# The normalisation's reciprocal root: from twelve VectorE instructions to a logarithm and an exponential on ScalarE and a Newton step on GpSimd

## The chip, the cores and the metric

The kernel runs on one core of a Trainium2 chip. The metric is the device time of one execution in microseconds (us); the time before is the median of three runs. The engines' names in the profile: PE is the tensor engine's matmuls and PEld its weight loads, DVE is VectorE, ACT is ScalarE, POOL is GpSimd, SP is SyncE, which issues most transfers. Each engine works through its own instructions in the order in which they were issued, and waits where an operand or a buffer isn't ready.

## What is computed

An attention over 8 batches of 12 heads, with 448 tokens and 64 columns a head, feeds a mixture of 8 experts. Queries and keys are normalised by their root mean square first:

```python
def rmsnorm(x, g):
    rms = np.sqrt(np.mean(x * x, axis=-1, keepdims=True) + 1e-06)
    return x / rms * g
q_n, k_n = (rmsnorm(q, g_q), rmsnorm(k, g_k))
scores = scale * np.matmul(q_n, k_n.transpose(0, 1, 3, 2))
scores = scores - np.max(scores, axis=-1, keepdims=True)
attn = np.exp(scores)
attn = attn / (np.sum(attn, axis=-1, keepdims=True) + 1e-09)
attn @ v
```

Then each of the 3584 tokens is given to the expert with the largest gate logit, and goes through that expert's two matrices with a relu between them. All is in float32, and the matmuls that need it split their operands in two parts.

## The kernel before

**Units and slots.** The attention works in 48 units of two heads (u = 0 to 47), and each unit in 7 slots, one for each chunk of 128 of the two heads' tokens. A slot issues the transposed scores of a chunk (`st`, L849), their exponential on ACT, and, for a unit two ahead, the plain scores of a chunk (`sa`, L821 and L816), of which DVE takes the row maxima (TENSOR_REDUCE at_hlw<-sa). Attention times values (`av`, L888), sums, gates and the transposes of finished rows lie between them. The PSUM pools of `st` and `sa` have two buffers each, so PE can be two chunks ahead of ACT's exponentials and of DVE's maxima.

**The normalisation.** For a unit to come, queries and keys are loaded (tile r), squared on ACT (`sumsq`, xrw<-r) and summed over 64 columns on DVE (TENSOR_REDUCE at_hlw<-xrw). The sums of three units make one group of 2 x 24 columns on 112 partitions. `rstd` computes 1/sqrt(sum/64 + 1e-6) of a group: on DVE, one instruction for the mean, two on integers for a first guess, and three Newton steps of three instructions each, so twelve. Eighteen such calls are made: five at the start on parts of groups (8, 16 or 24 columns for queries and as many for keys), thirteen later on whole groups of 48 columns. The result y is multiplied onto queries and keys by POOL (`norm`, xrw<-r,at_hlw), PE transposes what comes out (`tr`, L750), and ACT and DVE evacuate it into the matmul operands w1w, w2ha and xw, which SP's transfers complete (L763).

The sums, y and the scratch a and z of `rstd` are all views of one tile, at_hlw in the profile; the scratch has one buffer.

**The order of the work.** It is written by hand. A table (PLAN) sets the slot of each step: the squares of a unit 50 and 49 slots before its own start, `rstd` of a group 48 slots before its last unit, the norms 26 slots before a unit. A call that is "deferred" doesn't go out at once: its engine calls become items in a queue, and `pump` takes some 1 to 2 items per slot from it, from L52; other calls of these engines go out from L51. `rstd` goes into the queue `fast`. The routing of finished batches (one-hot of the largest logit, positions, slot tables: some 25 small DVE instructions a batch, also from L52) goes into the queue `slow`, which moves only while `fast` is empty. From unit 36 on three items go out per slot.

**After the attention** come the slots of the experts (ph at L480, py at L510), which PE fills without a break for most of the time, and an end of small slots that wait for indirect transfers.

**Other work of the engines in the attention.** ACT also squares, copies the transposes and evacuates av; POOL also adds up the exponentials (`csum`, r2w and others, 112 to 128 partitions by 448) and issues the indirect transfers of the routing.

Of the kernel before, what the change touches and what calls it, by code (L numbers as in the profile page):

```python
# [8 lines left out]
F32 = mybir.dt.float32  # L9
F32R = mybir.dt.float32r  # L10
I32 = mybir.dt.int32
AF = mybir.ActivationFunctionType
# [25 lines left out]
class Deferred:  # L38
    """Engine calls go out at once, or into the open queue."""
# [17 lines left out]
def deferred(fn):  # L57
    """What fn issues, as queue items."""
    Deferred.queue = items = []
    fn()  # L60
    Deferred.queue = None
    return items
# [3 lines left out]
def kernel(  # L66
# [16 lines left out]
    PE, SY = nc.tensor, nc.sync  # L83

# [8 lines left out]
    # ---------------------------------------------------------------- constants  # L93
# [22 lines left out]
    V.memset(half[64:128, 1:2], 1.0)  # L116
    V.memset(wg, 0.0)
# [61 lines left out]
    # ---------------------------------------------------------------- slot tables  # L179
# [20 lines left out]
    def tables(nm, ns, cnt, nb, taken, e_prev, half_blocks=None):  # L200
# [7 lines left out]
        if taken is not None:  # L208
            # blocks of at most half the size go last: columns of their own
            br = slice(NE, nv)  # L210
            nb_e = nb
            nb, cnt_e, cnt = tl("nb", [128, nv]), cnt, tl("cnt", [128, nv])
            V.scalar_tensor_tensor(out=nb[:, br], in0=nb_e, scalar=2.0, in1=half_blocks, op0=ALU.mult,
                                   op1=ALU.subtract)
            V.tensor_tensor(out=nb[:, ar], in0=nb_e, in1=nb[:, br], op=ALU.subtract)
            V.tensor_tensor(out=nb[:, ar], in0=nb[:, ar], in1=taken, op=ALU.subtract)
            for c in (ar, br):
                V.tensor_copy(out=cnt[:, c], in_=cnt_e)
# [44 lines left out]
        if taken is not None:  # L263
            # tokens of the slot
# [26 lines left out]
    def lists(nm, s0, ns, tb, two):  # L291
# [16 lines left out]
        def fin(a, n):  # L308
# [8 lines left out]
            if two:  # L317
                # the halves of a row
# [6 lines left out]
    # ---------------------------------------------------------------- storage  # L325
    # The same tiles serve the attention and then the experts.
# [13 lines left out]
    # These hold float32 first and then split operands.  # L340
# [21 lines left out]
    # 64 columns of zeros lie between the heads  # L362
# [13 lines left out]
    # one chunk of queries: 64 of each head, a block of rows and columns each  # L376
# [39 lines left out]
    # ---------------------------------------------------------------- experts  # L416
# [126 lines left out]
    def half_slot(s):  # L543
        """A slot of at most 128 tokens: these stay in the array, and the weights move."""
# [27 lines left out]
    def small_slot(s, xr):  # L572
        """A slot of at most 32 tokens, in a quarter of the array's columns: four column blocks at once."""
# [16 lines left out]
        # gate and row of a token, for each of its four pieces  # L590
# [49 lines left out]
    # ---------------------------------------------------------------- attention  # L640
    if True:
# [12 lines left out]
        def load_v(hb):  # L654
# [3 lines left out]
            # a partition's tokens lie next to each other, but for the middle chunk  # L658
# [48 lines left out]
        def rstd(hb, j0, j1):  # L707
            t = HB[hb]
            if "y" not in t:
# [5 lines left out]
            V.tensor_scalar(out=a, in0=t["ss"][:, :, sl], scalar1=1.0 / D, scalar2=1e-6,  # L715
                            op0=ALU.mult, op1=ALU.add)
            V.tensor_scalar(out=z.bitcast(I32), in0=a.bitcast(I32), scalar1=1,
                            scalar2=None, op0=ALU.arith_shift_right)
            V.tensor_scalar(out=y.bitcast(I32), in0=z.bitcast(I32), scalar1=-1,
                            scalar2=0x5F3759DF, op0=ALU.mult, op1=ALU.add)  # L720
            for _ in range(3):
                V.tensor_tensor(out=z, in0=y, in1=y, op=ALU.mult)
                V.scalar_tensor_tensor(out=z, in0=z, scalar=-0.5, in1=a,
                                       op0=ALU.mult, op1=ALU.mult)
                V.scalar_tensor_tensor(out=y, in0=z, scalar=1.5, in1=y,
                                       op0=ALU.add, op1=ALU.mult)
# [15 lines left out]
        def tr(u, g):  # L742
# [3 lines left out]
            # keys in their own order, queries by chunk of the load  # L746
# [55 lines left out]
        # Both heads' tokens on one axis, cut in chunks of 128: the middle one has an end of each.  # L802
        def columns(t, j):
            """Head and columns of the chunk's tokens."""
# [52 lines left out]
        def csum(u, h):  # L857
# [5 lines left out]
            # the middle chunk's rows of this head, and the first of its chunks  # L863
# [32 lines left out]
        # Four units at a time, each in its 32 columns of the array: the gate's products of both  # L896
        # heads in rows 0 to 15, the sums of the exponentials in rows 16 and 17.
# [153 lines left out]
        # slots between what gives the operands and the call  # L1051
# [39 lines left out]
        wps = ps_o.tile([128, 512], F32, tag="o", name="warm")  # L1091
        load(0)
# [5 lines left out]
        # engine calls of the slots to come, before and after the slot's exponential  # L1098
# [20 lines left out]
        # what each slot does; the first units follow each other more closely  # L1119
# [148 lines left out]
        # the last units' ends, among the first slot's products  # L1268
        after = []

        def go(*fs):
            """Issue the calls; what a call returns (evacuations) goes out after the next one."""
# [46 lines left out]
        # the slots: the next one's operands are made among the products of this one  # L1319
# [6 lines left out]
        for s in range(NSTAT):  # L1326
            # calls after the products of a beat
# [114 lines left out]
```

## Time and profile before

| | |
|---|---|
| median of 3 runs | 1171.19 us (1169.7 to 1174.05) |
| span of the profiled execution, first to last instruction | 1169.2 us |
| what lies between the median and this span | 2.0 us |
| mean granted clock of the tensor engine | 0.969 |
| start, until the first st | 38.1 us |
| attention, 48 units | 38.1 to 622 us |
| experts and end | 622 to 1169 us |

The page gives the busy time of each engine and its share of the span; a row of a group of instructions reads line, engine, operation, output<-inputs, shapes, count, busy us, mean ns of one, and the idle time of the engine ahead of them with what ended it. The profiled execution's own time isn't among the figures, only its span; the table sets the span against the median of the runs.

### The profile page before, as it was taken

To read this page: it belongs to the slowest core of one execution; us is meant where nothing else is said; L and a number is where in the kernel's file an instruction comes from. 1 tells how busy PE (TensorE), PEld (TensorE's weight loads), DVE (VectorE), ACT (ScalarE), POOL (GpSimd) and SP (SyncE) were. 2 spreads that over 40 slices of the span, in tenths; PEclk is the share of its full clock that TensorE was granted. 3 is DMA by queue.
4 is the path that set the end of the run, shared out by engine and by line. 5 is a ranking of instruction groups with operands and counts; after the bars stand their busy time and mean duration, and the time that the engine had idled before them with its cause. 6 is when DMAs were issued, how large, how long until landed. Compare 5 with 4: busy or idle time off the path is not lost.

```text
span 1169.2 us, 19997 instructions
## 1 busy us (share of the span) xinstructions
PE 1105.2 (95%) x6678; PEld 865.2 (74%) x6678; DVE 954.4 (82%) x1812; ACT 815.7 (70%) x1569; POOL 635.6 (54%) x575
## 2 busy tenths in 40 slices
PE   8899999999989999898899999999999999999993
PEld 6555665655556555455457898999999999999991
DVE  6987889999999999899978996778677777767770
ACT  6677878777767777575566764787666877667770
POOL 3467666777567775566665456533344324454340
PEclk8899999999999999898899999999999999999997
DMA  7655557666566665454354121111153111111260
GB/s 186 148 134 144 146 152 180 166 161 153 139 141 166 164 156 142 121 138 105 102 176 157 63 42 55 52 32 54 29 217 108 42 55 42 28 55 55 69 217 17
DMA packets 101345, 131.78 MB, mean 113 GB/s; under 512 B 29979, under 2 KB 95983, under 8 KB 99696
## 3 DMA queue, kind: packets, MB, share of 16 engines
q1 hardware_dynamic: 83588, 88.57, 30.2%
q0 software_dynamic: 17616, 41.80, 11.2%
q8 instruction: 57, 0.93, 0.4%
q14 instruction: 56, 0.46, 0.2%
q10 hardware_dynamic: 28, 0.01, 0.0%
HBM read 148.74 MB, written 22.38 MB: 146 GB/s over the span
## 4 chain that ended last, share of the span: by engine, by line
PE 65%; DVE 19%; DMA 6%; ACT 4%; issue 2%; POOL 1%; SPq 1%; ACTq 0%; DVEq 0%
PE ph L480 17%; PE py L510 16%; PE st L849 10%; PE av L888 9%; DVE at_hlw L51 4%; PE sa L821 4%; DMA lt<-l_d,tb_li 3%; DVE at_hlw L52 3%; DVE w1w L51 3%; DVE xw L51 2%; PE tr L750 2%; PE px L463 2%; PE xt L945 2%; DMA w1w<-xw 1%; PE sm L903 1%
## 5 line engine op out<-in xcount | busy, mean ns | idle before, releaser
L480 PE MATMUL ph<-xw,w1w 128*128 128x256 f32 x2016 | 247.5, 284 | 3.0 <-DVE hlw L51 2.3
L480 PEld LDWEIGHTS ph<-xw,w1w 128*128 128x128 f32 x2016 | 245.3, 193 | 5.1 <-DVE hlw L51 2.5
L51 DVE TENSOR_TENSOR w1w<-r,w1w 128x256 fp32r<-128x256 f32 x360 | 220.8, 671 | 14.1 <-ACT w1w L51 14.0
L51 ACT CAST w1w<-r 128x256 fp32r<-128x256 f32 x360 | 224.9, 726 | 0.0
L51 DVE TENSOR_REDUCE at_hlw<-sa 128x1 f32<-128x448 f32 x336 | 205.3, 615 | 17.0 <-PE sa L821 11.7
L849 PE MATMUL st<-w1w 128*128 128x448 f32 (+1 forms) x480 | 193.9, 453 | 1.9 <-ACT r2w L51 1.4
L849 PEld LDWEIGHTS st<-w1w 128*128 128x128 f32 (+1 forms) x480 | 108.2, 241 | 45.9 <-ACT r2w L51 19.3
L821 PE MATMUL sa<-w1w 128*128 128x448 f32 (+1 forms) x288 | 114.9, 400 | 22.6 <-DVE at_hlw L51 22.3
L51 POOL TENSOR_TENSOR r2w<-r2w 128x448 f32<-128x448 f32 (+1 forms) x72 | 82.6, 1148 | 81.1 <-DVE r2w L51 33.6
L51 ACT ACTIVATE hhw<-ph 128x512 fp32r<-128x512 f32 x56 | 33.5, 598 | 124.5 <-PE ph L480 124.5
L51 POOL TENSOR_TENSOR xrw<-r,at_hlw 112x512 f32<-112x512 f32 x95 | 97.6, 1048 | 36.9 <-PE tr L750 11.2
L510 PE MATMUL py<-w2lw,hhw 128*128 128x384 f32 x448 | 113.8, 334 | 0.0
L51 ACT ACTIVATE r2w<-st 128x448 f32<-128x448 f32 x168 | 89.3, 541 | 33.3 <-PE st L849 30.4
L849 PE MATMUL st<-w1w,w2ha 65*128 65x448 f32 x288 | 102.4, 376 | 0.0
L51 ACT ACTIVATE at_w2lw<-st 128x448 f32<-128x448 f32 x168 | 87.9, 540 | 12.1 <-PE st L849 10.3
L51 ACT CAST w1w<-tr 64x448 fp32r<-64x448 f32 x96 | 50.5, 526 | 65.3 <-DVE xw L51 64.7
L51 POOL DMA_INDIRECT out_dram<-yw,lb_oi x22 | 26.7, 1214 | 122.2 <-ACT yw L51 112.3
L51 POOL TENSOR_TENSOR r2w<-r2w,at_w2lw 64x448 f32<-64x448 f32 (+1 forms) x48 | 54.8, 1142 | 66.7 <-DVE r2w L51 38.9
L821 PEld LDWEIGHTS sa<-w1w 128*128 128x128 f32 (+1 forms) x288 | 56.9, 198 | 35.2 <-DVE at_hlw L51 32.4
L51 DVE SCALAR_TENSOR_TENSOR hlw<-ph,hhw 128x512 fp32r<-128x512 f32 x56 | 38.7, 691 | 53.2 <-ACT hhw L51 53.2
L510 PEld LDWEIGHTS py<-w2lw,hhw 128*128 128x128 f32 x448 | 80.9, 188 | 0.0
L51 ACT ACTIVATE w1w<-tr,gs 64x448 fp32r<-64x448 f32 x96 | 60.3, 628 | 29.1 <-DVE xw L51 28.4
(296 smaller groups left out, 2414.2 us busy)
## 6 DMA issues: line engine op xcount, KB each, us to landing
w1w<-xw SPq DMA_DIRECT2D x312, 112.0 KB
r<-in_q_dram SPq DMA_DIRECT2D x48, 224.0 KB
r<-in_k_dram SPq DMA_DIRECT2D x48, 224.0 KB
w2ha<-xw SPq DMA_DIRECT2D x72, 112.0 KB
x_d<-at_w2hb SPq DMA_DIRECT2D x8, 672.0 KB
x_d<-yw SPq DMA_DIRECT2D x8, 672.0 KB
r2w<-in_v_dram SPq DMA_DIRECT2D x16, 288.0 KB
at_w2lw<-in_v_dram SPq DMA_DIRECT2D x16, 288.0 KB
```

Of the source, the lines that this page charges most:

```text
L51: return fn(*a, **kw)
L52: Deferred.queue.append((self.kind, lambda: fn(*a, **kw)))
L463: PE.transpose(ps[:, i, 128 * t : 128 * t + 128], xr[t][:, 2 * g + i], idn)
L480: PE.matmul(ps[:, i], lhsT=lt_, rhs=rt_[:, c], start=n == 0, stop=n == 17)
L510: PE.matmul(ps[n][:, :384], lhsT=lt_[:, j, 128 * t : 128 * t + 128], rhs=rt_[:, 384 * n : 384 * n + 384], start=j == 0 and m == 0, stop=j ...
L750: PE.transpose(sp[:, c], src[:, c], idn[:CP, :CP])
L821: PE.matmul(ps[:, :S], lhsT=t["qq"][r, h, a : a + 128], rhs=t["kk"][h][r], start=True, stop=True)
L849: PE.matmul(ps[:, :S], lhsT=l, rhs=t["qq"][:, h] if first else t["ql"][:, h], start=first and (j != 3 or h == 0), stop=not first and (j != ...
L888: PE.matmul(t["av"][64 * h : 64 * h + 64, :S], lhsT=vv[r, u % 3, j], rhs=t["p"][r, j], start=c == 0, stop=c == 3)
L903: PE.matmul(R[g][32 * i : 32 * i + 32, :S], lhsT=sel[:, m], rhs=T[u + i // 2]["cs"][:, i % 2], start=m == 0, stop=False, tile_position=(0, ...
L945: PE.transpose(ps[:CP, 128 * c : 128 * c + 128], T[u]["xt"][:, c * CP : (c + 1) * CP], idn)
```

## The change

`rstd` keeps its inputs, its output and its place in the plan. The twelve DVE calls become two on ACT and five on POOL. The logarithm is taken of sum/64 times 2^-44 plus 1e-6 times 2^-44, the exponential of -1/2 times that, less 22 ln 2, which takes the factor back out. One Newton step on POOL follows: a = sum/64 + 1e-6, z = y*y, z = z*a, z = 1.5 - z/2, y = y*z. Two constants for the activations' bias (tile lnb) are set at the start on DVE. POOL's calls go through a new Deferred object (GP), so that they are queue items as well. A call names the table set "natural_log_exp_and_others" for ACT ahead of the first load.

```diff
+    GP = Deferred(nc.gpsimd, "op")
...
+    lnb = cp.tile([128, 2], F32, name="lnb")
+    V.memset(lnb[:, 0:1], 1e-6 * 2.0**-44)
+    V.memset(lnb[:, 1:2], -22.0 * math.log(2.0))
...
             y = t["y"][:, :, sl]
-            V.tensor_scalar(out=a, in0=t["ss"][:, :, sl], scalar1=1.0 / D, scalar2=1e-6,
-                            op0=ALU.mult, op1=ALU.add)
-            V.tensor_scalar(out=z.bitcast(I32), in0=a.bitcast(I32), scalar1=1,
-                            scalar2=None, op0=ALU.arith_shift_right)
-            V.tensor_scalar(out=y.bitcast(I32), in0=z.bitcast(I32), scalar1=-1,
-                            scalar2=0x5F3759DF, op0=ALU.mult, op1=ALU.add)
-            for _ in range(3):
-                V.tensor_tensor(out=z, in0=y, in1=y, op=ALU.mult)
-                V.scalar_tensor_tensor(out=z, in0=z, scalar=-0.5, in1=a,
-                                       op0=ALU.mult, op1=ALU.mult)
-                V.scalar_tensor_tensor(out=y, in0=z, scalar=1.5, in1=y,
-                                       op0=ALU.add, op1=ALU.mult)
+            ss = t["ss"][:, :, sl]
+            A.activation(out=z, in_=ss, func=AF.Ln, scale=2.0**-44 / D, bias=lnb[:CP, 0:1])
+            A.activation(out=y, in_=z, func=AF.Exp, scale=-0.5, bias=lnb[:CP, 1:2])
+            GP.tensor_scalar(out=a, in0=ss, scalar1=1.0 / D, scalar2=1e-6, op0=ALU.mult, op1=ALU.add)
+            GP.tensor_tensor(out=z, in0=y, in1=y, op=ALU.mult)
+            GP.tensor_tensor(out=z, in0=z, in1=a, op=ALU.mult)
+            GP.tensor_scalar(out=z, in0=z, scalar1=-0.5, scalar2=1.5, op0=ALU.mult, op1=ALU.add)
+            GP.tensor_tensor(out=y, in0=y, in1=z, op=ALU.mult)
...
+        A.preload_act_table_set("natural_log_exp_and_others")
```

In the changed kernel the deferred calls go out from L53 and the others from L52.

The order of the instructions shows what moves. First ACT at the very start, before: two squares of each of units 0, 1 and 2, then the first evacuation of a transpose (w1w<-tr).

```order
L51 ACT_TABLE_LOAD
L51 ACTIVATE xrw_132<-r1_1_131 112x512
L51 ACTIVATE xrw_132<-r1_0_130 112x512
L51 ACTIVATE xrw_132<-r1_1_131 112x512
L51 ACTIVATE xrw_132<-r1_0_130 112x512
L51 ACTIVATE xrw_132<-r1_1_131 112x512
L51 ACTIVATE xrw_132<-r1_0_130 112x512
L51 ACTIVATE w1w_133<-tr0_1_216,gs_78 64x448 x2
```

And of the change, from the same place:

```order
L52 ACT_TABLE_LOAD
L52 ACTIVATE xrw_135<-r1_1_134 112x512
L52 ACTIVATE xrw_135<-r1_0_133 112x512
L52 ACTIVATE xrw_135<-r1_1_134 112x512
L52 ACTIVATE xrw_135<-r1_0_133 112x512
L53 ACTIVATE at_hlw_144<-at_hlw_144,lnb_89 112x16
L53 ACTIVATE at_hlw_144<-at_hlw_144,lnb_89 112x2x8
L52 ACTIVATE xrw_135<-r1_1_134 112x512
L52 ACTIVATE xrw_135<-r1_0_133 112x512
L53 ACTIVATE at_hlw_144<-at_hlw_144,lnb_89 112x32
L53 ACTIVATE at_hlw_144<-at_hlw_144,lnb_89 112x2x16
L52 ACTIVATE w1w_136<-tr0_1_215,gs_78 64x448 x2
```

The logarithm and the exponential of unit 0 stand behind the squares of unit 1, and those of units 1 and 2 ahead of the first evacuation. Each list has this one table load and no other.

Second, DVE in the steady part, while it takes the row maxima of unit 12 (at_hlw<-sa12); the rows at_hlw<-at_hlw of 48 columns are a root. Before:

```order
L51 TENSOR_REDUCE at_hlw_141<-sa12_3_1759 128x1
L52 TENSOR_SCALAR at_hlw_141<-at_hlw_141 112x48
L51 TENSOR_TENSOR xw_134<-tr13_0_1761,xw_134 128x448
L52 TENSOR_TENSOR at_hlw_141<-at_hlw_141 112x48
L51 TENSOR_REDUCE at_hlw_141<-sa12_4_1779 128x1
L52 SCALAR_TENSOR_TENSOR at_hlw_141<-at_hlw_141 112x48
L51 TENSOR_TENSOR yw_137<-xt4_1783,rs1_144 112x4x128
L52 SCALAR_TENSOR_TENSOR at_hlw_141<-at_hlw_141 112x48
L51 TENSOR_REDUCE at_hlw_141<-sa12_5_1804 128x1
L52 TENSOR_TENSOR at_hlw_141<-at_hlw_141 112x48
L51 TENSOR_REDUCE at_hlw_141<-sa12_6_1818 128x1
```

Of the change:

```order
L52 TENSOR_REDUCE at_hlw_144<-sa12_3_1728 128x1
L52 TENSOR_TENSOR xw_137<-tr13_0_1730,xw_137 128x448
L52 TENSOR_REDUCE at_hlw_144<-sa12_4_1748 128x1
L52 TENSOR_TENSOR yw_140<-xt4_1752,rs1_147 112x4x128
L52 TENSOR_REDUCE at_hlw_144<-sa12_5_1773 128x1
L52 TENSOR_REDUCE at_hlw_144<-sa12_6_1787 128x1
L53 TENSOR_REDUCE lo0_1794<-at_hlw_144 112x32
```

The root's rows are gone from between the maxima, and the first row of the routing (lo0) stands there already. Counted over the whole order, the routing's one-hot matmuls of batches 0 to 5 come one to three units earlier on PE; the routing's and tables' rows that DVE has in units 36 to 43 were 8, 0, 16, 6, 0, 16, 21 and 15, and are 3, 9, 10, 3, 9, 21, 21 and 1. SP's order is the same.

Third, POOL at a place of the same kind: norms (xrw) and adds of exponentials (r2w, at_w2lw). Before:

```order
L51 TENSOR_TENSOR xrw_132<-r1_0_130,at_hlw_141 112x2x4x64
L51 TENSOR_TENSOR xrw_132<-r1_1_131,at_hlw_141 112x2x4x64
L51 TENSOR_TENSOR r2w_135<-at_w2lw_139 128x448
L51 TENSOR_TENSOR r2w_135<-r2w_135,at_w2lw_139 64x448
L51 TENSOR_TENSOR at_hhw_140<-r2w_135,at_w2lw_139 128x448
L51 TENSOR_TENSOR r2w_135<-r2w_135,at_w2lw_139 128x448
```

Of the change:

```order
L52 TENSOR_TENSOR xrw_135<-r1_0_133,at_hlw_144 112x2x4x64
L52 TENSOR_TENSOR xrw_135<-r1_1_134,at_hlw_144 112x2x4x64
L53 TENSOR_SCALAR at_hlw_144<-at_hlw_144 112x48
L52 TENSOR_TENSOR r2w_138<-at_w2lw_142 128x448
L53 TENSOR_TENSOR at_hlw_144<-at_hlw_144 112x48 x2
L52 TENSOR_TENSOR r2w_138<-r2w_138,at_w2lw_142 64x448
L53 TENSOR_SCALAR at_hlw_144<-at_hlw_144 112x48
L52 TENSOR_TENSOR at_w2lw_142<-r2w_138,at_w2lw_142 128x448
L53 TENSOR_TENSOR at_hlw_144<-at_hlw_144 112x48
L52 TENSOR_TENSOR r2w_138<-r2w_138,at_w2lw_142 128x448
```

The five steps stand between the adds, one or two at a time; each adds to POOL's row, and the second waits for ACT's exponential.

More of the change, by code (lines that the diff above doesn't have):

```diff
@@ L1 @@
+import math
 from contextlib import ExitStack
```

## The prediction

> **What bounds the kernel now.** I read the page first: the engines' busy shares and the chain that ended last.
>
> ```profile
> span 1169.2 us, 19997 instructions
> PE 1105.2 (95%) x6678; PEld 865.2 (74%) x6678; DVE 954.4 (82%) x1812; ACT 815.7 (70%) x1569; POOL 635.6 (54%) x575
> PE 65%; DVE 19%; DMA 6%; ACT 4%; issue 2%; POOL 1%; SPq 1%; ACTq 0%; DVEq 0%
> PE ph L480 17%; PE py L510 16%; PE st L849 10%; PE av L888 9%; DVE at_hlw L51 4%; PE sa L821 4%; DMA lt<-l_d,tb_li 3%; DVE at_hlw L52 3%; DVE w1w L51 3%; DVE xw L51 2%; PE tr L750 2%; PE px L463 2%; PE xt L945 2%; DMA w1w<-xw 1%; PE sm L903 1%
> ```
>
> PE carries the chain, but 19% of it runs over DVE, and 3% (some 35 us) over "DVE at_hlw L52". L52 is the place from which queued work is issued, and at_hlw written there by DVE is this very root. To find where it binds I cut the span into the start, the attention and its end; each row of a window gives its length, then PE, PEld, DVE, ACT and POOL busy in us (and instructions), the granted clock, the share of DMA and GB/s. The second fence has the same stretches for the st matmuls alone (L849); a unit (two heads) issues 16 of them, so the counts give units.
>
> ```profile
> 0.00:38.10 38.10, 31.58 (x187) 27.46 (x188) 26.80 (x83) 25.37 (x94) 14.28 (x30) 0.87 0.72 181
> 38.10:77.80 39.70, 33.34 (x143) 20.42 (x141) 36.94 (x71) 26.73 (x63) 23.57 (x22) 0.87 0.51 126
> 87.50:233.40 145.90, 145.90 (x767) 87.27 (x765) 128.41 (x258) 116.96 (x252) 99.86 (x91) 1.00 0.62 158
> 233.40:463.40 230.00, 220.84 (x1134) 131.23 (x1132) 219.56 (x433) 169.63 (x370) 157.12 (x145) 0.99 0.62 151
> 463.40:580.80 117.40, 103.34 (x482) 59.98 (x480) 107.14 (x223) 68.33 (x150) 74.44 (x70) 0.90 0.46 114
> 580.80:622.00 41.20, 41.20 (x219) 24.74 (x217) 31.18 (x55) 30.33 (x61) 29.83 (x26) 1.00 0.56 171
> ```
>
> ```profile
> 38.10:77.80 39.70, 17.02 (x48) 10.76 (x48) 0.87 0.51 126
> 87.50:233.40 145.90, 67.83 (x208) 43.25 (x208) 1.00 0.62 158
> 233.40:463.40 230.00, 100.27 (x304) 63.72 (x304) 0.99 0.62 151
> 463.40:580.80 117.40, 44.16 (x128) 27.88 (x128) 0.90 0.46 114
> ```
>
> From 87.5 to 233.4 us PE is busy all the time, at the full granted clock, while DVE is busy 128 of 146 us. That is the floor: 208/16 = 13 units in 145.9 us, 11.22 us each, and a lighter DVE can bring nothing there. Above the floor stand three stretches. The first three units take 39.7 us, 6.0 over 3 x 11.22. The next 304/16 = 19 units take 230.0, 16.8 over 213.2; DVE is busy 95% of it. Then 128/16 = 8 units take 117.4, 27.6 over 89.8, and the clock falls to 0.90 because PE waits. In all **50.4 us** are DVE's doing. After 580.8 PE is full again and no root is left; the experts behind it stay as they are.
>
> How much of it is the root's? Single units show that. The first five rows below are the longest units that hold a root (7 of its 12 instructions or all); the next two hold no root, only routing work (L52 too); the last holds 7 of a root's as well.
>
> ```profile
> 257.80:271.70 13.90, 12.13 (x54) 7.39 (x52) 13.07 (x24) 9.71 (x22) 9.61 (x9) 0.88 0.58 113
> 330.30:345.70 15.40, 12.99 (x62) 7.43 (x60) 14.57 (x25) 10.12 (x23) 9.77 (x10) 0.89 0.58 108
> 403.90:416.40 12.50, 10.74 (x54) 6.61 (x52) 11.67 (x20) 9.60 (x23) 9.22 (x9) 1.00 0.62 121
> 480.80:496.40 15.60, 13.69 (x66) 8.01 (x65) 14.58 (x26) 9.48 (x22) 9.60 (x9) 0.89 0.39 92
> 521.00:537.60 16.60, 13.62 (x67) 7.79 (x65) 15.35 (x27) 9.46 (x21) 11.74 (x12) 0.89 0.27 63
> 463.40:480.80 17.40, 14.57 (x62) 8.24 (x60) 14.61 (x25) 9.20 (x21) 10.16 (x10) 0.80 0.66 168
> 550.50:567.30 16.80, 14.23 (x63) 7.67 (x61) 15.13 (x37) 7.69 (x17) 9.56 (x9) 0.80 0.49 130
> 294.80:306.70 11.90, 11.90 (x68) 7.04 (x64) 10.93 (x26) 8.56 (x19) 7.66 (x7) 1.00 0.49 124
> ```
>
> Over 11.2 us the five stand 2.7, 4.2, 1.3, 4.4 and 5.4 us, together 18.0; the two routing units 6.2 and 5.6. The last, at 11.9, hardly stands over it: a root alone does not stall PE, it does so where DVE is full besides (13.1 of 13.9 us busy in the first row) and where it meets a run of POOL work, as shown next.
>
> **What is removed.** The root's instructions on DVE, by the groups of instructions:
>
> ```profile
> L52 DVE TENSOR_SCALAR at_hlw<-at_hlw 112x48 int32<-112x48 int32 (+5 forms) x54 | 42.0, 777 | 0.4
> L52 DVE SCALAR_TENSOR_TENSOR at_hlw<-at_hlw 112x48 f32<-112x48 f32 (+2 forms) x108 | 37.1, 344 | 1.5
> L52 DVE TENSOR_TENSOR at_hlw<-at_hlw 112x48 f32<-112x48 f32 (+2 forms) x54 | 19.9, 368 | 0.8
> ```
>
> Eighteen roots of 12 instructions: 216, and 42.0 + 37.1 + 19.9 = 99.0 us of DVE. That is far more than 48 columns need, and the order of time shows why:
>
> ```profile
> 484.92 2.04 POOL L51 TENSOR_TENSOR xrw<-r,at_hlw 112x512 f32<-112x512 f32 x2
> 485.05 3.27 DVE L52 TENSOR_SCALAR at_hlw<-at_hlw 112x48 f32<-112x48 f32 x2
> 486.92 1.12 POOL L51 TENSOR_TENSOR r2w<-at_w2lw 128x448 f32<-128x448 f32 x1
> 488.98 0.21 DVE L52 TENSOR_TENSOR at_hlw<-at_hlw 112x48 f32<-112x48 f32 x1
> 489.22 1.89 DVE L52 SCALAR_TENSOR_TENSOR at_hlw<-at_hlw 112x48 f32<-112x48 f32 x1
> ```
>
> Two small instructions last 3.27 us and end only as a run of POOL instructions ends; the next takes 0.21 us with POOL quiet. So DVE stands still behind POOL, with the row maxima that PE's next sa needs queued behind it. These stalls go with the instructions. Late next is PE itself, at the floor, and in some units DVE's routing work, which keeps such stalls.
>
> **What is added.** ACT gets 36 small instructions, POOL 90, DVE two memsets at the start (nothing). Nearest rows:
>
> ```profile
> L52 ACT ACTIVATE lo<-lo 112x32 f32<-112x32 f32 x7 | 1.6, 231 | 0.1
> L51 ACT ACTIVATE xw<-tr,gs 128x448 fp32r<-128x448 f32 x48 | 30.2, 629 | 3.6 <-PE tr L750 3.4
> 34.57 0.20 POOL L51 TENSOR_TENSOR at_hlw<-xrw 112x8 f32<-112x8 f32 x1
> 32.10 2.39 POOL L51 TENSOR_TENSOR xrw<-xrw 112x256 f32<-112x256 f32 x5 [13.10 <-ACT xrw L51]
> ACT w1w L51 <- DVE xw L51: 93.0, 90, 5.2
> L51 ACT ACT_TABLE_LOAD x1 | 1.3, 1283 | 0.8 <-PEq L1428 0.8
> ```
>
> An activation of 48 columns lies between 0.23 (32 columns) and 0.63 us (448); it is nearest to the first, so 0.25: 36 x 0.25 = 9 us of ACT in all. ACT is idle 230.0 - 169.6 = 60 us in the 19 units, 3.2 us each; a root's 0.5 us per three units hides there. On POOL a dependent step lies between 0.20 (8 columns) and 2.39/5 = 0.48 us (mean of 256 down to 16); I take 0.3. Five make 1.5 us per root, 27 us in all (18 to 43), against 230.0 - 157.1 = 73 us idle in the 19 units, 11 per root: hidden too. Neither addition can gain by itself, since it only adds work; without its cover each would cost its own 9 or 27 us.
>
> Two waits are new. The logarithm waits in ACT's queue for DVE's sum of squares; behind it stand the exponentials of st, for which PE waits two tiles later (two buffers). In the steady part it is issued a slot after that sum, so I charge nothing; the bounds are nothing and, by the wait row above (ACT for DVE), a mean of 93.0/90 = 1.03 us, inside the 3.2. POOL's second instruction waits for ACT's exponential; behind it stand the adds for the sums and the norms, which have units of lead. SP's queue is unchanged.
>
> At the **start** ACT is not free:
>
> ```profile
> 6.38 0.59 DVE L52 TENSOR_SCALAR at_hlw<-at_hlw 112x16 f32<-112x16 f32 x3
> 8.33 1.15 ACT L51 ACTIVATE xrw<-r 112x512 f32<-112x512 f32 x2 [2.78 <-DMA r<-in_k_dram]
> 8.94 2.04 POOL L51 TENSOR_TENSOR xrw<-r,at_hlw 112x512 f32<-112x512 f32 x2 [2.83 <-DVE at_hlw L52]
> 11.84 1.25 ACT L51 ACTIVATE w1w<-tr,gs 64x448 fp32r<-64x448 f32 x2
> ```
>
> The first root ran on DVE from 6.38 and the norms from 8.94. Now the logarithm stands behind the squares of unit 1, which wait for a load until 8.33 and end at 9.48. Two activations (0.5) and four POOL steps (1.2) end at 11.2: the norms start 2.2 us late, and the second root's pair stands before the first evacuation (11.84). The root of units 3 to 5 gives part of it back. I charge 2 us, between 0 and 4.
>
> **The sum.** The five root units: 18.0, less about 2 for routing left in them, 16 (11 to 18). The other 16.8 - 8.2 = 8.6 us of the 19 units: half, 4.5, since the roots' last instructions and routing share them (2 to 8). The other 27.6 - 9.8 = 17.8 of the eight: 3 (0 to 8); here routing, which moves up into freed places, still fills two units. The first three units: 5 of 6.0 (3 to 6). Less 2 at the start: **26.5 us** saved, bounds 12 to 40. The profiled span of 1169.2 becomes 1142.7; the median 1171.2 lies 2.0 above the span, so 1144.7, say **1144.5**.
>
> **Rivals.** *Routing takes over*: with the root gone its instructions sit closer, and stall behind POOL in the same way. For it: 6.2 and 5.6 us over in units without a root. Half of the five units' 16, none of the rest but 5.5 early, less 2: about 12 saved, 1159. *All of DVE's excess goes but the two routing units and the start*: 50.4 - 11.8 - 2 = 36.6 saved, 1134.5; for it the 35 us of the root in the chain. *ACT binds instead*, no change, about 1170: against it, 74% busy where DVE is at 95%. *Slower*: the logarithm holds ACT's queue for a late DVE sum, PE starves for exponentials. Price: what exceeds 3.2 us of ACT's idle time a unit, 18 times; it decides when the mean hold passes 3.2 + 26.5/18 = 4.7 us. At the longest such wait seen, 5.2, it loses 18 x 2.0 = 36 and ends at 1180.7. *Not what it says*: if the two functions needed a table load each, 36 x 1.283 = 46 us more on ACT, 1191 with none hidden; but the changed order lists one load, as before.
>
> The Trainium skill ("ScalarE: Activation LUTs", Table sets) puts a change of set at about 2.66 us with its drain, 96 us for 36 and 1240 in all with nothing hidden, and names one set with both functions; the one row of a load here, 1.283 us, agrees with its load alone.
>
> **Chances.** Forecast (savings of 20 to 33) 0.55; routing 0.22; all of it 0.12; no change 0.06; slower 0.05 (table loads 0.01 of it). Range 1130 to 1162: it takes in the forecast, nearly all of the routing case and most of the best one. A measurement of this kernel tells about 0.5%, 6 us, from no change: faster by more 0.89, within 0.06, slower 0.05.
>
> **What would show it.** DVE's at_hlw rows of L52 gone; the stretches behind 233.4 nearer 11.2 us a unit, at a full clock; idle of PE's sa behind DVE at_hlw much smaller; the first norms near 11 us. Wrong if ACT's rows for lnb show waits of microseconds, if POOL's 48-column steps last over 1 us, or if routing rows stretch where the root stood.

## The result, and the profile after

| | before | after |
|---|---|---|
| median, us | 1172.62 (4 runs, 1169.7 to 1177.33) | 1144.11 (4 runs, 1139.65 to 1144.52) |
| span of the profiled execution, us | 1169.2 | 1137.9 |
| mean granted clock | 0.969 | 0.980 |

The ratio is 0.9748, with a 95% interval of 0.97 to 0.9796: faster by 28.5 us in the medians. The prediction said 1144.5. The profiled execution of the changed kernel took 1139.65 us and was the shortest of its four, so a sum made on the two spans, 31.3 us, is some 3 us more than the medians give.

Two lines of the page of the changed kernel, span and busy times:

```profile
span 1137.9 us, 19896 instructions
PE 1089.8 (96%) x6678; PEld 856.9 (75%) x6678; DVE 863.7 (76%) x1598; ACT 827.7 (73%) x1605; POOL 656.8 (58%) x665
```

DVE lost 954.4 - 863.7 = 90.7 us of busy time and 214 instructions (216 of the roots less two memsets); ACT got 12 and POOL 21 us. PE's busy time fell too, by 15.4 us with the same 6678 matmuls: matmuls that run at half clock count longer, and there are fewer of those.

The stretches of the prediction, cut at the first st of the same units (start; units 0 to 2; unit 3; 4 to 16; 17 to 35; 36 to 43), in the changed kernel. Columns as before: length, PE, PEld, DVE, ACT and POOL busy, granted clock, DMA share, GB/s:

```profile
0.00:37.70 37.70, 29.12 (x187) 25.96 (x188) 20.00 (x49) 25.98 (x91) 16.29 (x44) 0.91 0.73 178
37.70:77.70 40.00, 34.44 (x144) 21.28 (x142) 26.50 (x47) 28.84 (x75) 27.09 (x33) 0.83 0.50 120
87.40:233.40 146.00, 145.53 (x768) 87.03 (x766) 114.44 (x216) 119.94 (x263) 107.88 (x118) 1.00 0.64 158
233.40:454.00 220.60, 217.35 (x1134) 129.90 (x1132) 185.39 (x351) 174.14 (x382) 167.83 (x178) 0.99 0.66 157
454.00:550.30 96.30, 93.62 (x483) 54.98 (x481) 82.50 (x191) 70.23 (x153) 71.92 (x75) 0.98 0.60 140
```

Against the rows of before: the start 38.1 to 37.7; the first three units 39.7 to 40.0, no gain; units 4 to 16 145.9 to 146.0, the floor as foretold; units 17 to 35 230.0 to 220.6; units 36 to 43 117.4 to 96.3, more than two thirds of the whole gain in 8 of 48 units. In the four stretches of the attention PE's idle time (length less PE) went from 6.4 + 0 + 9.2 + 14.1 = 29.7 to 5.6 + 0.5 + 3.3 + 2.7 = 12.1 us. The clock gave back the rest: length times (1 - granted clock) is 5.2 + 0 + 2.3 + 11.7 = 19.2 before and 6.8 + 0 + 2.2 + 1.9 = 10.9 after. Together the stretches are 30.1 us shorter. These two numbers explain some 26 of that: 18 were waits, and 8 a lower granted clock.

The five units that held a root, at the new places:

```profile
257.70:267.90 10.20, 10.20 (x54) 6.50 (x52) 8.67 (x18) 9.33 (x22) 8.49 (x11) 1.00 0.57 139
327.60:338.70 11.10, 11.10 (x62) 6.64 (x61) 8.56 (x17) 9.46 (x22) 9.02 (x13) 1.00 0.59 146
398.10:408.40 10.30, 10.30 (x55) 6.54 (x53) 8.77 (x19) 9.43 (x22) 8.56 (x12) 1.00 0.58 139
465.80:477.10 11.30, 11.30 (x62) 6.74 (x61) 9.15 (x22) 9.65 (x22) 8.00 (x12) 1.00 0.68 163
500.30:512.50 12.20, 11.74 (x63) 6.74 (x62) 8.34 (x21) 8.87 (x20) 9.28 (x13) 1.00 0.49 106
```

They took 74.0 us and take 55.1: 18.9 saved. Four have PE busy from end to end at a full clock. DVE, busy 11.7 to 15.4 us in each before, is busy 8.3 to 9.2.

The groups of instructions that the change adds, and two that waited for the root (line, engine, operation, count | busy, mean ns | idle before and what ended it); the last row is the matmuls sa in the kernel before:

```profile
L53 ACT ACTIVATE at_hlw<-at_hlw,lnb 112x48 f32<-112x48 f32 (+2 forms) x36 | 11.7, 326 | 1.5 <-DVE at_hlw L52 0.9
L53 POOL TENSOR_TENSOR at_hlw<-at_hlw 112x48 f32<-112x48 f32 (+2 forms) x54 | 15.9, 294 | 11.9 <-ACT at_hlw L53 9.8
L53 POOL TENSOR_SCALAR at_hlw<-at_hlw 112x48 f32<-112x48 f32 (+2 forms) x36 | 8.1, 224 | 9.9 <-DVE at_hlw L52 5.6 <-DVE bs L53 2.4 <-DVE gs L52 0.4
L823 PE MATMUL sa<-w1w 128*128 128x448 f32 (+1 forms) x288 | 110.6, 385 | 8.9 <-DVE at_hlw L52 5.8 <-DMA w1w<-xw 2.6 <-issue 0.3
L52 POOL TENSOR_TENSOR xrw<-r,at_hlw 112x512 f32<-112x512 f32 x95 | 97.4, 1045 | 2.5 <-PE tr L752 2.2
L821 PE MATMUL sa<-w1w 128*128 128x448 f32 (+1 forms) x288 | 114.9, 400 | 22.6 <-DVE at_hlw L51 22.3 <-ACT w1w L51 0.3
```

ACT's pair costs 0.33 us an instruction where 0.25 was taken, and waits 1.5 us for all 36: the wait that the slower rival needed is not there. POOL's 90 steps come to 15.9 + 8.1 = 24.0 us, 0.27 each (taken: 0.3). PE's idle time ahead of sa is 8.9 us, 5.8 of it behind DVE; it was 22.6, 22.3 of it behind DVE.

### The profile page after: what moved, and what is told of

It reads as the page before. It is cut to its first block, busy times and chain, and to the rows that moved or that the text cites. A ratio compares the mean times of both kernels' runs of the same rounds, so it can differ in the third digit from the quotient of the medians.

```text
span 1137.9 us, 19896 instructions
## 1 busy us (share of the span) xinstructions
PE 1089.8 (96%) x6678; PEld 856.9 (75%) x6678; DVE 863.7 (76%) x1598; ACT 827.7 (73%) x1605; POOL 656.8 (58%) x665
## 3 DMA queue, kind: packets, MB, share of 16 engines
q0 software_dynamic: 17616, 41.80, 11.7%
## 5 line engine op out<-in xcount | busy, mean ns | idle before, releaser
L52 DVE TENSOR_REDUCE at_hlw<-sa 128x1 f32<-128x448 f32 x336 | 206.9, 618 | 48.3 <-PE sa L823 30.0
L52 DVE TENSOR_TENSOR w1w<-r,w1w 128x256 fp32r<-128x256 f32 x360 | 221.0, 672 | 13.8 <-ACT w1w L52 13.5
L52 ACT CAST w1w<-r 128x256 fp32r<-128x256 f32 x360 | 224.8, 722 | 0.0
L851 PEld LDWEIGHTS st<-w1w 128*128 128x128 f32 (+1 forms) x480 | 107.3, 239 | 45.1 <-ACT r2w L52 21.2
L52 ACT ACTIVATE hhw<-ph 128x512 fp32r<-128x512 f32 x56 | 33.5, 598 | 121.8 <-PE ph L485 121.8
L52 POOL TENSOR_TENSOR r2w<-r2w 128x448 f32<-128x448 f32 (+1 forms) x72 | 82.4, 1144 | 68.4 <-DVE r2w L52 30.6
L52 ACT ACTIVATE r2w<-st 128x448 f32<-128x448 f32 x168 | 90.0, 541 | 40.7 <-PE st L851 35.7
L823 PE MATMUL sa<-w1w 128*128 128x448 f32 (+1 forms) x288 | 110.6, 385 | 8.9 <-DVE at_hlw L52 5.8
L52 ACT ACTIVATE at_w2lw<-st 128x448 f32<-128x448 f32 x168 | 89.3, 540 | 13.4 <-PE st L851 11.6
L52 POOL TENSOR_TENSOR xrw<-r,at_hlw 112x512 f32<-112x512 f32 x95 | 97.4, 1045 | 2.5 <-PE tr L752 2.2
L52 POOL DMA_INDIRECT out_dram<-yw,lb_oi x22 | 28.3, 1286 | 122.0 <-ACT yw L52 118.9
L52 DVE SCALAR_TENSOR_TENSOR hlw<-ph,hhw 128x512 fp32r<-128x512 f32 x56 | 38.7, 691 | 51.9 <-ACT hhw L52 51.9
L52 ACT ACTIVATE w1w<-tr,gs 64x448 fp32r<-64x448 f32 x96 | 60.3, 629 | 23.0 <-DVE xw L52 22.3
L52 POOL TENSOR_TENSOR r2w<-r2w,at_w2lw 64x448 f32<-64x448 f32 (+1 forms) x48 | 54.9, 1144 | 38.0 <-DVE r2w L52 19.5
L851 PEld LDWEIGHTS st<-w1w,w2ha 65*128 65x128 f32 x288 | 70.9, 246 | 5.4 <-DMA r2w<-in_v_dram 2.7
L52 ACT ACTIVATE xrw<-r 112x512 f32<-112x512 f32 (+1 forms) x124 | 64.6, 526 | 9.7 <-DMA r<-in_k_dram 7.2
```

What stands on the lines that cost most here:

```text
L52: return fn(*a, **kw)
L823: PE.matmul(ps[:, :S], lhsT=t["qq"][r, h, a : a + 128], rhs=t["kk"][h][r], start=True, stop=True)
L851: PE.matmul(ps[:, :S], lhsT=l, rhs=t["qq"][:, h] if first else t["ql"][:, h], start=first and (j != 3 or h == 0), stop=not first and (j != ...
```

## Experiments

The chain of the change has two sides that the diff does not part. DVE loses the roots (theory one). And a root is 7 queue items in place of 12, so that the routing behind it in the queue is issued up to three units earlier, on PE, DVE and POOL (the rival). Medians and ratios are against runs of the kernel before on the same chip.

**The root moved, the order kept.** Five empty items fill each root up to 12, which puts the routing back where it stood:

```diff
             GP.tensor_tensor(out=y, in0=y, in1=z, op=ALU.mult)
+            Deferred.queue.extend([("op", lambda: None)] * 5)
```

> The changed kernel with five empty items behind each root in the queue, so that a root takes 12 items again: PE's, DVE's and SP's other work stands in the order of the kernel before, only the root is on ACT and POOL. Theory (DVE's freed time is the gain): 1141 to 1149 us, some 25 to 30 us under the kernel before, and no stalled units of 14 us and more but those of routing. Rival (the gain comes from the routing that moves up because the queue is shorter): 1158 us or more, half of the gain or less.

**The order alone.** The kernel before, with its twelve DVE instructions packed into 7 items, so that the routing moves up as in the changed kernel:

```diff
+            o = [fn for _, fn in Deferred.queue]
+            Deferred.queue[:] = [("op", lambda f=f: [x() for x in f]) for f in
+                [o[2 * i : 2 * i + 2] for i in range(5)] + [o[10:11], o[11:12]]]
```

> The kernel before with its twelve DVE instructions packed in seven queue items: the order of PE and of the routing is that of the changed kernel, the root is on DVE as before. Theory (DVE's freed time): 1165 to 1178 us, no gain to speak of, and the root's rows on DVE still near 99 us. Rival (routing moves up): 1145 to 1158 us.

Measured: e1_pad 1151.35 us (4 runs), ratio 0.9799 (0.9754 to 0.9845); e2_dve7 1166.35 (10 runs), 0.9929 (0.9903 to 0.9955); the kernel before 1173.93 (13 runs). The root moved alone is worth 22.6 us, the order alone 7.6, together 30.2: about what both give at once. Neither theory holds alone: e1_pad came between its two ranges, 2.4 us over the first, and e2_dve7, inside its first range, is still faster with an interval that leaves 1 out. By these medians three quarters are DVE's relief and one quarter the routing's place. The windows say more. Units 17 to 35, then 36 to 43, of e1_pad:

```profile
233.60:451.00 217.40, 215.57 (x1135) 129.53 (x1133) 184.30 (x354) 174.18 (x382) 165.73 (x175) 1.00 0.67 160
451.00:562.70 111.70, 99.00 (x483) 56.93 (x481) 98.78 (x197) 69.53 (x154) 76.17 (x79) 0.94 0.50 120
```

and of e2_dve7:

```profile
239.50:477.10 237.60, 224.00 (x1134) 132.18 (x1132) 208.34 (x426) 171.87 (x371) 158.47 (x146) 0.97 0.61 146
477.10:577.50 100.40, 93.03 (x482) 54.85 (x480) 88.98 (x215) 69.04 (x150) 69.45 (x65) 1.00 0.56 134
```

In the old order, taking the root off DVE saves 230.0 - 217.4 = 12.6 us in the 19 units and only 5.7 in the eight, where routing goes on stalling. In the new order with the root still on DVE the eight units gain 117.4 - 100.4 = 17.0, and the 19 units lose 7.6. With both, the eight have the gain (96.3), and the 19 lose only 220.6 - 217.4 = 3.2 of what the root gave.

The 7.6 us of e2_dve7 in the medians are not the order's alone. Its items hold two instructions of the root each, so that a root is through in one unit where it lay in two before (11 of its 12 instructions in unit 7, in place of 7). Units 7 and 10, in which no routing instruction stands yet, are 1.2 and 0.9 us longer for it, and units 4 to 16 together 6.6. How much of the loss of the 19 units is this packing, and how much routing that meets the roots, no run parts.

**Both orders mixed.** Empty items only for groups up to 12, whose roots go out before unit 32:

```diff
+            if hb < 13:
+                Deferred.queue.extend([("op", lambda: None)] * 5)
```

> The changed kernel with the five empty items behind the roots of units 0 to 38 alone: the routing of the first batches stands as in the kernel before, that of the last ones moves up. Theory (moving the routing pays in the last twelve units alone, 111.7 against 96.3 us for units 36 to 43, and costs 3 us in the 19 units ahead of them, 217.3 against 220.7, by transfers that now fall together): 1138 to 1142 us, with no wait of sa for a transfer near unit 22. Rival (the two parts don't add up, since the last routing depends on where the earlier one ends): 1146 to 1152 us.

Measured: 1138.22 us (6 runs, 1134.98 to 1147.82), ratio 0.9706 (0.9663 to 0.9749). The two stretches:

```profile
231.20:448.80 217.60, 215.73 (x1134) 129.65 (x1132) 185.18 (x358) 174.20 (x382) 166.60 (x176) 1.00 0.67 160
448.80:549.30 100.50, 96.67 (x483) 56.23 (x481) 82.58 (x194) 70.85 (x154) 75.23 (x78) 0.95 0.66 134
```

The 19 units are as in e1_pad (217.4), the eight stand much nearer to the changed kernel (96.3) than to e1_pad (111.7). That is the two orders' effects in their places; the gain over the changed kernel lies inside the intervals.

**The Newton step on DVE.** GP becomes V in the five calls; seven items, so the order of the changed kernel:

```diff
-            GP.tensor_scalar(out=a, in0=ss, scalar1=1.0 / D, ...)
+            V.tensor_scalar(out=a, in0=ss, scalar1=1.0 / D, ...)
...
-            GP.tensor_tensor(out=y, in0=y, in1=z, op=ALU.mult)
+            V.tensor_tensor(out=y, in0=y, in1=z, op=ALU.mult)
```

> Logarithm and exponential on ACT, the five instructions of the Newton step on DVE in place of POOL: 90 instructions of DVE come back of 216. Theory (the gain goes with DVE's time at the root): they take 90/216 of 99 us, some 41 us, and 40% of the 28 us of gain go: 1152 to 1160 us. First rival (POOL's steps cost as much as they save): 1140 to 1146 us. Second rival (any root on DVE that meets a run of POOL work stalls PE for long): 1165 us or more.

Measured: 1151.53 us (4 runs, 1145.2 to 1157.33), ratio 0.9818 (0.9764 to 0.9873). Its groups:

```profile
L53 DVE TENSOR_TENSOR at_hlw<-at_hlw 112x48 f32<-112x48 f32 (+2 forms) x54 | 23.4, 434 | 4.8 <-ACT at_hlw L53 4.2
L53 DVE TENSOR_SCALAR at_hlw<-at_hlw 112x48 f32<-112x48 f32 (+2 forms) x36 | 15.5, 430 | 0.2
```

38.9 us of DVE work come back, of 99.0, and the time gives up some 7 to 9 of 28.5. The same steps take 0.43 us on DVE here in the mean, and 0.22 to 0.29 on POOL. The median lies a little under what was expected. The interval overlaps that of the changed kernel's first runs (0.97 to 0.9796) and lies clear of that of its second ones (e9 below, 0.9697 to 0.9753), so the direction, that DVE time in this kernel costs, holds; the share of 40% is not shown.

**The table set not named.** The call that names it is left out:

```diff
-        A.preload_act_table_set("natural_log_exp_and_others")
```

> The changed kernel without the call that names the table set: the order of ACT has 37 table loads in place of one, two for each root. 36 times 1.283 us are 46 us more of ACT. Theory (ACT has 3.2 us idle in a unit and takes them): 1144 to 1152 us. Rival (a load stands ahead of an exponential for which PE waits): 1165 to 1191 us; by the Trainium skill's 2.66 us a switch up to 1240 us.

Measured: 1194.66 us (4 runs, 1183.53 to 1196.26), ratio 1.0141 (1.0071 to 1.0211): slower than before. The groups of loads, the stretch of units 4 to 16, and one root there in order of time:

```profile
L53 ACT ACT_TABLE_LOAD x25 | 32.1, 1283 | 1.6 <-DVE at_hlw L52 1.2
L52 ACT ACT_TABLE_LOAD x12 | 15.4, 1283 | 1.0 <-PEq L1430 0.8
```

```profile
104.80:265.00 160.20, 150.57 (x767) 88.29 (x765) 114.97 (x216) 131.99 (x273) 108.91 (x119) 0.98 0.59 144
```

```profile
215.81 1.28 ACT L53 ACT_TABLE_LOAD   x1
217.46 1.28 ACT L52 ACT_TABLE_LOAD   x1
218.75 0.54 ACT L52 ACTIVATE at_w2lw<-st 128x448 f32<-128x448 f32 x1
219.34 0.60 PE L851 MATMUL st<-w1w 128*128 128x448 f32 x1 [2.28 <-ACT at_w2lw L52]
```

37 loads in place of one: 36 x 1.283 = 46 us of ACT, and by the ratios (1.0141 - 0.9748) x 1173.9 = 46 us of time; by the two intervals it can be some 32 to 60. No part of it is seen to be hidden, even in the 13 units that stood at the floor: 160.2 where the floor is 146.0, though ACT is busy 132 of it. Each stretch of the trace grows by the time of its loads or more: the start by 12.1 us for 6 further loads, the first three units by 5.3 for 4, units 4 to 16 by 14.2 for 10, units 17 to 35 by 16.0 for 12, units 36 to 43 by 6.6 for 4. The rows show why: two loads stand ahead of an exponential, and PE waits 2.28 us for it, so ACT's idle time elsewhere is no cover. This is the rival "not what it says" of the prediction, 1191; that it comes so near is luck within the interval. By the Trainium skill ("ScalarE: Activation LUTs", What ACT_TABLE_LOAD costs) some 1.38 us of drain come with each load, by estimate 96 us in all for 36; no such loss shows here.

**What the Newton step costs.** First without it, five empty items in its place:

```diff
-            GP.tensor_scalar(out=a, ...)
...
-            GP.tensor_tensor(out=y, in0=y, in1=z, op=ALU.mult)
+            Deferred.queue.extend([("op", lambda: None)] * 5)
```

> The changed kernel with the Newton step left out (y is what the two activations give) and five empty items in its place in the queue, so that the other work stands as in the padded kernel e1_pad. Theory (POOL's five steps lie beside its idle time): 1147 to 1153 us, within 4 us of e1_pad's 1151.4. Rival (the steps hold POOL's adds and norms up, or DVE's routing behind them): 1145 us or less.

The expectation miscounts: two activations and five empty items make seven, so the order is that of the changed kernel and not of e1_pad, and the theory's 1151.4 is no yardstick. Measured: 1137.53 us (7 runs), ratio 0.9683 (0.9653 to 0.9713). Then a second Newton step, four POOL calls more, and so 11 items:

> The changed kernel with a second Newton step: nine POOL instructions a root in place of five, 72 more, some 18 us more of POOL. Theory (POOL has 11 us idle a root in the steady part): 1142 to 1147 us, as the changed kernel. Rival (POOL's steps are on the way of the norms or of DVE): 1150 us or more.

Measured: 1156.75 us (6 runs), ratio 0.9849 (0.9816 to 0.9882), 12.6 over the changed kernel's median. That looked like a price of POOL work, but its 11 items also put the order back. So the same with the nine POOL calls packed into five items:

```diff
+            o = [fn for _, fn in Deferred.queue]
+            Deferred.queue[3:] = [("op", lambda f=f: [x() for x in f]) for f in
+                                  [o[2 * i + 3 : 2 * i + 5] for i in range(4)]]
```

> The second Newton step again (72 more POOL instructions, 20 us of POOL), packed so that a root takes 7 queue items as in the changed kernel: the order of all other engines is that of the changed kernel. Theory (a POOL step costs about a quarter of its time: 90 of them left out in e4_no_newton, which has 7 items as the changed kernel, brought 6.6 us): 4 to 7 us over the changed kernel run beside it, about 1150 us. Rival (e7_pool2's 12.6 us over the changed kernel came from the steps, not from its 11 items): 10 us or more over it, 1154 us or more.

Beside it on one chip ran the changed kernel again, and five POOL steps of the same shape on a tile that nobody reads, with the second factor of y left out:

> The changed kernel once more, as the yardstick of the three below on the same chip: 1141 to 1147 us.

> The five POOL steps are issued at the same places but work on a scratch tile of their own, so that nothing waits for them but POOL's own queue; y is what the activations give, and the Newton step is left out of what is computed. If the steps cost by the time that they take on POOL (and by holding up DVE's routing rows): as the changed kernel, 1142 to 1147 us. If they cost by the chain from ACT's exponential to the norms: as without them, 1136 to 1140 us.

Measured: e10 1141.93 us (6 runs), 0.9716 (0.9688 to 0.9743); e9 1142.15 (6 runs), 0.9725 (0.9697 to 0.9753); e11 1143.07 (5 runs), 0.9724 (0.9695 to 0.9753). The groups of e10:

```profile
L53 POOL TENSOR_TENSOR at_hlw<-at_hlw 112x48 f32<-112x48 f32 (+2 forms) x108 | 31.1, 288 | 17.1 <-ACT at_hlw L53 10.5
L53 POOL TENSOR_SCALAR at_hlw<-at_hlw 112x48 f32<-112x48 f32 (+2 forms) x54 | 14.0, 259 | 9.9 <-DVE at_hlw L52 4.9 <-DVE bs L53 1.9
```

72 more steps, 45.1 us of POOL in place of 24.0, cost nothing that can be measured when the order stays, where 4 to 7 us were expected: the loss of e7 was the order's. Taking the five steps away (e4) gave 4.6 to 6.6 us in the medians all the same. Moving them out of the chain (e11) gave nothing, so it would be their work and not their place; but then e10 should have lost. The intervals of e4 (up to 0.9713) and e9 (from 0.9697) overlap, and this stays open.

**The best of both.** No Newton step, 12 items a root up to group 12, and 7 behind:

```diff
+            Deferred.queue.extend([("op", lambda: None)] * (10 if hb < 13 else 5))
```

> No Newton step (left out of what is computed), and empty items so that a root takes 12 items in units 0 to 38 and 7 later: the two gains of e4_no_newton (6.6 us) and e8_pad_mid (5.9 us) together. If they add: 1130 to 1134 us. If both remove the same stalls: 1136 to 1139 us.

Measured: 1137.13 us (5 runs, 1134.49 to 1139.19), ratio 0.9681 (0.9652 to 0.971), against 0.9683 of e4 and 0.9706 of e8: the two small gains do not add. Between e8 and e12, which differ in the Newton step alone, lie 1.1 us in the medians and 2.9 by the ratios, with intervals that overlap: no price of the step shows there. The median of e12 is the shortest of all, with a root that is less exact; with the computation unchanged that is e8, 1138.22, not shown to be faster than the changed kernel.

**The start.** Roots of group 0 on DVE as before, all others as changed:

```diff
+            if hb == 0:
...
+                return
```

> The changed kernel, but the two roots of the first three units stay on DVE as before; the other sixteen are on ACT and POOL. Theory for the first units (they gained nothing since the logarithm stood behind a late load at the start, the row of maxima then left PE's queue 1.7 us later, into the loads of the values, and PE waited 2.5 us and lost the full clock): the norms start near 9 us again, no wait of st for a transfer near 38 us, the first three units take 34 to 37 us in place of 40.0, and the whole 1138 to 1142 us. Rival (these units are bound by transfers and the clock anyway): 39 to 41 us, and 1143 to 1147 us.

Measured: 1142.08 us (6 runs), ratio 0.9728 (0.9693 to 0.9763), as the changed kernel. In its trace the first st comes at 36.1 us in place of 37.7, and the first three units take 41.7 in place of 40.0: together 77.8 against 77.7. The norms start at 8.90 us there, as hoped, but st still waits 1.74 us behind a transfer, and the 34 to 37 us for the first three units did not come. The second trace of the changed kernel (e9) has 38.6 + 41.6 = 80.2 for the same stretch, so that two microseconds here are not clear of what differs from run to run.

## Why the prediction was right, and where its steps were not

The total was right: 26.5 us were foretold and 28.5 measured in medians. That it came so near is in part luck: two steps gave 5.3 us less than foretold each, others 9.4, 2.9 and 2.4 more, and these cancel. By step, on the spans:

| step | foretold, us | measured, us |
|---|---|---|
| five root units | -16 | -18.9 |
| the other 16 of units 17 to 35 | -4.5 | +0.8 |
| the other 6 of units 36 to 43 | -3 | -12.4 |
| first three units | -5 | +0.3 |
| start | +2 | -0.4 |
| units 4 to 16 | 0 | +0.1 |
| all else | 0 | -0.8 |
| sum | -26.5 | -31.3 |

Each measured term comes from one trace. The second trace of the changed kernel (e9) has 38.6 us in the start, 41.6 in the first three units, 146.4, 218.7 and 98.1 in the others, so a term is good to some 2 us.

**The five root units** were right in mechanism and size: DVE's stalls went with its instructions, and PE runs at the floor there. e1_pad shows it with the order held: these units take 57.2 us there, in place of 74.0.

**The other six of the eight** are the step that was mis-sized: "routing, which moves up into freed places, still fills two units", 3 us with a bound of 8. It does not fill both of them. Unit 36, 17.4 us before, is 11.8 long, and the other routing unit (42, 16.8) 11.8 too; unit 41 has become the long one, 12.9 before:

```profile
512.50:528.10 15.60, 14.03 (x65) 7.20 (x64) 15.17 (x38) 8.34 (x19) 10.14 (x10) 0.89 0.30 67
```

The order listed the routing's rows of both units (8 and 21 before, 3 and 21 now), and the prediction read it as work that only changes its place. But it is the place that counts: unit 42 is 5.0 us shorter with as many rows. In the kernel before, four routing instructions in these eight units stretch to 2.1 to 3.8 us beside POOL's norms and adds, as the root's did. One of them in unit 36, POOL beside it, the sa that waits for it, and the one in unit 42:

```profile
469.01 2.04 POOL L51 TENSOR_TENSOR xrw<-r,at_hlw 112x512 f32<-112x512 f32 x2
469.05 3.15 DVE L52 TENSOR_TENSOR lo<-lo,rmx 112x32 f32<-112x32 f32 x1
472.79 0.74 PE L816 MATMUL sa<-xw 128*128 128x448 f32 x1 [2.83 <-DVE at_hlw L51]
554.38 3.51 DVE L52 TENSOR_TENSOR ta_px<-ta_px 128x6 f32<-128x6 f32 x1
```

e1_pad, with the old order, has the same two at 3.17 and 3.54 us. In the changed kernel the longest routing instruction of the eight units is this one:

```profile
533.88 1.78 DVE L53 SCALAR_TENSOR_TENSOR ta_js<-ta_js,ta_eb 128x3 f32<-128x3 f32 x1
```

With the order held (e1_pad) these six units take 87.8 us, 2.6 more than before; so all that they gained is the order's. e2_dve7 shows what the place is worth, 17.0 us in these eight units with the root still on DVE.

**The other 16 units** gave nothing (1.3 us in e9's trace), where half of 8.6 was foretold. The root's own excess did go as foretold where the order was held: in e1_pad these 16 units take 184.0 in place of 188.2. But the earlier routing brought a stall that was not there before, in unit 22. Windows of 3 us around it, and the wait:

```profile
281.00:284.00 3.00, 3.00 (x16) 1.50 (x15) 1.86 (x4) 2.64 (x7) 2.92 (x4) 1.00 1.04 176
284.00:287.00 3.00, 3.00 (x17) 1.88 (x16) 2.27 (x4) 2.48 (x6) 2.75 (x4) 1.00 1.09 289
287.00:290.00 3.00, 3.00 (x18) 1.75 (x21) 2.54 (x6) 2.69 (x8) 1.90 (x2) 1.00 1.06 225
290.00:293.00 3.00, 1.86 (x11) 0.83 (x4) 0.64 (x2) 1.89 (x4) 1.20 (x2) 0.96 0.46 97
293.00:296.00 3.00, 3.00 (x12) 1.78 (x13) 1.82 (x4) 1.66 (x3) 2.02 (x3) 0.50 0.59 164
```

```profile
292.71 0.64 PE L823 MATMUL sa<-w1w 128*128 128x448 f32 x1 [1.11 <-DMA w1w<-xw]
```

The DMA engines are full for 9 us (share 1.04 to 1.09); the operand w1w of sa comes late; PE waits 1.1 us, and has half its clock behind that. Unit 22 takes 14.9 us there, and 13.4, 13.8 and 13.2 in e9, e10 and e11, which have the same order and a wait of 0.9 to 1.4 us for the same transfer; in e1_pad and e8_pad_mid, in the other order, it takes 11.7 and has no such wait. That the stall goes with the order is shown. That the routing's indirect transfers are what fills the DMA is the likely reason: the changed kernel issues one at 284.40, among these loads, where e1_pad issues none from 267 to 312 and its DMA is full for 6 us. No run moves these transfers alone. The prediction spoke of SP's queue as unchanged, which holds, and did not ask when POOL's transfers go out.

**The first three units** failed as a step. The 6.0 us over the floor were put down to DVE, which was busy 36.9 of 39.7. It is busy 26.5 of 40.0 now, and the time is the same. DVE's waits were real, and they did shrink. PE's idle time ahead of sa in these units, before and after:

```profile
L821 PE MATMUL sa<-w1w 128*128 128x448 f32 x18 | 8.0, 445 | 4.5 <-DVE at_hlw L51 4.5
L823 PE MATMUL sa<-w1w 128*128 128x448 f32 x18 | 7.9, 438 | 2.3 <-DVE at_hlw L52 1.7 <-DMA w1w<-xw 0.6
```

In their place comes a wait of st that was not there before, and a transfer ends it:

```profile
37.25 0.63 SPq L668 DMA_DIRECT2D r2w<-in_v_dram  x1
37.27 1.41 ACTq L52 DMA_DIRECT2D w1w<-xw  x1
...
40.70 0.71 PE L851 MATMUL st<-w1w,w2ha 65*128 65x448 f32 x1 [2.48 <-DMA r2w<-in_v_dram]
```

```profile
37.70:40.20 2.50, 0.52 (x4) 0.23 (x2) 0.47 (x1) 1.42 (x12) 1.90 (x2) 1.00 0.79 185
40.20:47.00 6.80, 6.30 (x19) 5.17 (x20) 3.06 (x5) 5.43 (x17) 3.27 (x7) 0.50 0.71 174
```

The second st waits 2.48 us among the loads of the values, and 6.8 us at half clock stand beside it. In e1_pad, e4, e11 and e12 the same st waits 1.6 to 2.4 us, put down there to the transfer of its own operand w1w. The prediction took the whole excess as gone with DVE's load, and did not ask what PE would wait for next. The nine traces that have no root on DVE and a single table load take 37.0 to 41.6 us here, 39.4 in the mean.

**The start** was right in its steps and wrong in its end. As foretold, the pair stands behind the squares of unit 1, the norms start at 11.22 us and the evacuation late, at 14.42 in place of 11.84:

```profile
9.32 0.63 ACT L53 ACTIVATE at_hlw<-at_hlw,lnb 112x16 f32<-112x16 f32 x2
10.03 0.51 POOL L53 TENSOR_TENSOR at_hlw<-at_hlw 112x16 f32<-112x16 f32 x2 [3.34 <-ACT at_hlw L53]
...
11.22 2.04 POOL L52 TENSOR_TENSOR xrw<-r,at_hlw 112x512 f32<-112x512 f32 x2
...
14.42 0.61 ACT L52 ACTIVATE w1w<-tr,gs 64x448 fp32r<-64x448 f32 x1
```

But the first st came no later, 37.7 us against 38.1; what sets it is not shown. With the old root there (e5_mixed) it came at 36.1, and by unit 3 nothing of that was left.

**The additions** cost nothing that shows, as foretold, at 0.33 and 0.27 us an instruction. With twice the POOL work this still holds (e10); whether the last 5 us of e4 are theirs is open.

## What to carry to other kernels

Where work goes through one shared queue, taking items from it also moves everything behind them: run the change with the queue's length kept, and the queue's change without the rest, before a gain is put down to the engine that was relieved. An engine that is full beside a stall may be its cause and the stall still not go with it; read the row of the instruction that waited, and ask what it would wait for next. And a cheap instruction on an engine with idle time is only free where nothing that another engine waits for is queued behind it: 36 table loads found no cover on an engine that was idle a quarter of the time.

## What the runs showed of the hardware

- **A wait of one to three microseconds can cost clock.** In unit 22 PE stood still for 1.1 us after a stretch in which it was busy all the time (3.00 of 3.00 in three windows), and the clock fell to 0.50. The Trainium skill ("TensorE: Matmul & The Clock Gate", HAM oscillation) gives as its rule that PE should not be idle for over some 3.4 us; here the clock fell beside waits of 1.1 and 2.5 us. Not every such wait does it: PE's idle time in the trace of before has one of 1.75 us at 410.6 behind which the clock stayed full, and the wait in unit 22 is 1.4 us long in e9 without a fall, where the unit takes 13.4 us in place of 14.9.
- **A step of 16 to 48 columns is slower on DVE than on POOL in the mean alone.** The rows of e3 (DVE) and of the changed kernel (POOL) give the shortest, the median and the longest in ns:

```profile
L53 DVE TENSOR_TENSOR at_hlw<-at_hlw x54: 174/208/1173, 10.3 to 516.1; 112x48 f32<-112x48 f32 x42, 112x16 f32<-112x16 f32 x6, 112x32 f32<-112x32 f32 x6
L53 POOL TENSOR_TENSOR at_hlw<-at_hlw x54: 217/278/797, 10.0 to 509.3; 112x48 f32<-112x48 f32 x42, 112x16 f32<-112x16 f32 x6, 112x32 f32<-112x32 f32 x6
```

  The middle one takes 0.21 us on DVE and 0.28 on POOL; the mean is 0.43 against 0.29, since some on DVE last far longer, up to 1.17 us here. A routing instruction on DVE reached 3.51 us beside POOL's norms.
